# Pooled attention values accumulated onto the local ones in PSUM, for the jobs of the first batch half

## The chip, the cores and the metric

The kernel runs on one core of a Trainium2 chip. The metric is device time in microseconds for one execution, median of several runs. TensorE is called PE here, VectorE DVE, ScalarE ACT, GpSimd POOL; SP is the engine that issues the DMAs, from one queue that it works off in order. PE, DVE, ACT and POOL also run their own instructions in order.

## What is computed

Two attentions are added, and the sum goes through two feed-forward blocks. The attentions, from the reference (B = 2, H = 8, S = 576, D = 64, factor 4):

```python
q_d = q.reshape(B, H, Sd, factor, D).mean(axis=3)
...
out_d = sm_attn(q_d, k_d, v_d)
out_up = np.repeat(out_d, factor, axis=2)
...
out_local = np.matmul(attn, v)
return (out_up + out_local).astype(np.float32)
```

The pooled attention has 144 queries and keys, and each of its output rows is repeated for four neighbouring queries. The local attention sees keys less than four positions away. The sum, 1152 tokens of 512 channels, goes through `g = h * sigmoid(h); g @ w_out` (2048 hidden channels) and then through four experts of 1024 hidden channels, weighted by normalised `domain_probs`.

## The kernel before, in words

**Jobs.** Attention is cut into 16 jobs: two batches `b`, two chunks `c` of the sequence (256 and 320 queries, 4 and 5 blocks of 64), four pairs of heads `hp`. Jobs 0 to 7 are b = 0 (jobs 0 to 3 have 256 queries, jobs 4 to 7 have 320), jobs 8 to 15 are b = 1. After the fourth job of each batch a small tail job takes the last 16 pooled queries of all eight heads. A job goes through `local_scores`, `local_max`, `local_exp`, `down_scores`, `norm`, `trans`, `values` and `split_x`, one step a tick, three ticks a job.

**values and split_x.** `values` writes one PSUM tile `o`, of which there is one (`o_p`, bufs=1). Its columns 320 and up take the pooled result of 64 or 80 columns (line 408: four fp32 matmuls, two heads by two halves of the keys), its first 256 or 320 columns the local result (line 412: one fp32 matmul for each block and head). ACT copies the pooled part to SBUF with the factor 0.25 (`od`, line 415), DVE adds it onto the local part, each column for four queries (line 417). `split_x` then writes the sum in two parts for the feed-forward products, `xh` on ACT (line 424) and the rest `xl` on DVE (line 425), after which `o` is free for the next job.

**Weights.** The weights of the first feed-forward block come as 32 pieces of 512 KB through three staging buffers (`stg`, line 156). Two ACT instructions (lines 181 and 182) and two of DVE (183 and 187) decode a piece; DVE's line 187 is the last reader of its staging buffer. ACT then writes the upper part into `wbuf` (line 189), POOL the lower part (line 190). Twelve hidden-product tiles of a chunk need the first eight pieces; the second product of that chunk (`g2_step`) takes one more piece for each of its eight hidden blocks. These eight pieces are called f0 to f7 below; in the names of the order before they are stg64_546, 555, 564, 661, 670, 733, 753 and 789, in that of the order after stg64_537, 546, 555, 649, 658, 718, 738 and 774.

**Who sets the order.** The code gives each instruction a priority, and a scheduler of the framework sets the order of every engine's queue from the priorities and its own estimate of times. One instruction that changes its length or goes away can thus move others, on all queues, DMA issues among them.

**Products.** All products of the feed-forward blocks go through line 487 (first block, and the first product of the experts) and line 693. In the trace an fp32 matmul of the attention shows as two records, so four matmuls of line 408 are "x8" and eight of line 412 are "x16".

Of the kernel before, what the change touches and what calls it, by code (L numbers as in the profile page):

```python
# [15 lines left out]
ACTF = mybir.ActivationFunctionType  # L16
# [10 lines left out]
WIN = BQ + 6  # L27
# [32 lines left out]
def attention_moe_kernel(ctx, tc, kqa, kqb, qtl, va, vb, w64, w1d, w2d, dpr, out):  # L60
    nc = tc.nc
    PE, ACT, DVE, POOL, SP = nc.tensor, nc.scalar, nc.vector, nc.gpsimd, nc.sync
# [246 lines left out]
    def after(i, earlier):  # L309
        follow(i, earlier, "PSUM bank")  # L310
# [52 lines left out]
    def norm(j):  # L363
# [5 lines left out]
            DVE.tensor_tensor(out=j.sm, in0=j.lo, in1=j.st[:, 13:13 + nb].unsqueeze(2).to_broadcast([128, nb, WIN]), op=ALU.mult)  # L369
        ACT.activation(out=j.ed, in_=j.ed, func=ACTF.Copy, scale=j.st[:, 13 + nb:14 + nb])  # L370

    def trans(j):
        nb = j.nb
        if j.c == 1 and j.hp == 0:
            atd[j.b] = ac.tile([72, 2, NH, 80], F32, tag="atd1", name="atd1")
        t1 = t_p.tile([128, 4, 128], F32, tag="t1", name="t1")
        t2 = t_p.tile([128, 4, 128], F32, tag="t2", name="t2")
        j.at = ac.tile([WIN, 5, 128], F32, tag="at", name="at")
        for m in range(nb):
            PE.transpose(t1[0:WIN, m] if m < 4 else t2[0:WIN, 0], j.sm[:, m, :], ident)  # L380
        for kh in range(2):
            PE.transpose(t2[0:72, 1 + kh], j.ed[:, 72 * kh:72 * kh + 72], ident)
        ACT.activation(out=j.at[:, 0:4], in_=t1[0:WIN], func=ACTF.Copy)
        if nb == 5:
            ACT.activation(out=j.at[:, 4], in_=t2[0:WIN, 0], func=ACTF.Copy)
            dst = atd[j.b][:, :, 2 * j.hp:2 * j.hp + 2, 0:64]
        else:
            j.atd = ac.tile([72, 2, 2, 64], F32, tag="atd0", name="atd0")
            dst = j.atd
        ACT.activation(out=dst, in_=t2[0:72, 1:3].rearrange("p a (h q) -> p a h q", h=2), func=ACTF.Copy)  # L390

    def tail_trans(l):
        t2 = t_p.tile([128, 4, 128], F32, tag="t2", name="t2")
        for kh in range(2):
            PE.transpose(t2[0:72, 1 + kh], l.ed[:, 72 * kh:72 * kh + 72], ident)
        ACT.activation(out=atd[l.b][:, :, :, 64:80], in_=t2[0:72, 1:3].rearrange("p a (h q) -> p a h q", q=16),
                       func=ACTF.Copy)

    def values(j):
        b, hp, n, nb = j.b, j.hp, j.n, j.nb  # L400
        nd = n // 4
        o = o_p.tile([128, 512], F32, tag="o", name="o")
        v = vd[b, hp]
        for h in range(2):
            p = slice(64 * h, 64 * h + 64)
            for kh in range(2):
# [542 lines left out]
```

## Time and profile before

| | |
|---|---|
| median of 3 runs | 689.73 us (688.86 to 691.73) |
| profiled execution | 695.09 us, of which its span 693.1 us |
| PE busy | 658.0 us, 95% of the span |
| DVE busy | 441.9 us, 64% |
| ACT busy | 333.0 us, 48% |
| POOL busy | 247.2 us, 36% |
| mean granted PE clock | 0.974 of full |

The profile's page gives each engine's busy time; a view by stretches gives the same for parts of the span; the chain of waits follows the work that ended last back to the start; the view in order of time lists an engine's instructions, with the idle time before each and what ended it in brackets. A busy PE is not a PE at its peak: matmuls overlap, so the time that a run of them takes is read from the chain, where each piece lasts until the next one starts.

### The profile page before, as it was taken

Reading aid. Unit: us, or ns where it says so; the run is one execution under the profiler, and the core shown is the slowest. Engines: PE = TensorE matmul, PEld = TensorE weight load, DVE = VectorE, ACT = ScalarE, POOL = GpSimd, SP = SyncE. Lnnn points to the kernel's source line nnn. Section 1 sums busy time; section 2 is a strip of 40 time slices with the busy share of each in tenths; the row PEclk is TensorE's granted clock in tenths of the full one; section 3 lists DMA queues with packets and bytes.
Section 4 is the critical chain, followed back from the end, with each engine's and each line's share of the span. In section 5 each row is a group of like instructions: output and inputs, shape, how many; then the busy total and the mean of one; then the engine's idle time right before and its main releaser. Section 6 shows DMA issues by size and latency. Waiting matters only on the chain.

```text
span 693.1 us, 13803 instructions
## 1 busy us (share of the span) xinstructions
PE 658.0 (95%) x5516; PEld 641.0 (92%) x5516; DVE 441.9 (64%) x882; ACT 333.0 (48%) x753; POOL 247.2 (36%) x346
## 2 busy tenths in 40 slices
PE   5878779999999999999999999999999999999996
PEld 3758669998999999999999999999999999999996
DVE  5578967638564644585665985548855669756444
ACT  4659666647664533444335643345533356433321
POOL 5344762114240000154265432456232654322210
PEclk9597989999999999999999999999999999999999
DMA  9655553105250210022001410004310020000001
GB/s 288 203 160 173 168 178 99 27 7 152 93 183 1 61 62 2 1 100 115 1 2 53 130 61 1 1 2 122 92 31 1 1 61 1 1 32 17 16 31 45
DMA packets 16927, 48.16 MB, mean 69 GB/s; under 512 B 2976, under 2 KB 4256, under 8 KB 16864
## 3 DMA queue, kind: packets, MB, share of 16 engines
q1 hardware_dynamic: 16864, 47.29, 22.0%
q8 instruction: 43, 0.70, 0.4%
q14 instruction: 20, 0.16, 0.1%
HBM read 44.93 MB, written 2.36 MB: 68 GB/s over the span
## 4 chain that ended last, share of the span: by engine, by line
PE 83%; DMA 7%; DVE 6%; ACT 1%; POOL 1%; issue 1%; SPq 0%; ACTq 0%; POOLq 0%; DVEq 0%
PE mm L487 53%; PE p L693 26%; DMA stg<-in_w_dram 4%; DMA vg<-in_va_dram 2%; DVE dec L187 1%; DVE gl L513 1%; DVE dec L183 1%; PE s L320 1%; PE o L412 1%; PE t L380 1%; PE o L408 1%; DVE acc L721 1%; POOL vg L257 0%; PE s L344 0%; ACT stg L182 0%
## 5 line engine op out<-in xcount | busy, mean ns | idle before, releaser
L487 PE MATMUL mm<-xh,wbuf 128*128 128x256 f32 (+2 forms) x1280 | 268.9, 297 | 3.3 <-ACT xh L424 2.4
L487 PEld LDWEIGHTS mm<-xh,wbuf 128*128 128x128 f32 x1280 | 211.5, 190 | 4.1 <-ACT xh L424 3.0
L487 PE MATMUL mm<-xl,wbuf 128*128 128x256 f32 (+2 forms) x640 | 190.0, 297 | 0.0
L675 POOL TENSOR_TENSOR r<-r 128x128 f32<-128x128 f32 x160 | 93.4, 596 | 182.9 <-ACT r L669 143.3
L678 DVE TENSOR_TENSOR h<-r,h 128x384 fp32r<-128x384 f32 (+1 forms) x128 | 91.8, 719 | 64.0 <-ACT h L677 63.7
L487 PEld LDWEIGHTS mm<-xl,wbuf 128*128 128x128 f32 x640 | 121.7, 190 | 0.1
L677 ACT ACTIVATE h<-r 128x384 fp32r<-128x384 f32 (+1 forms) x128 | 73.3, 577 | 84.4 <-POOL r L675 54.3
L487 PE MATMUL mm<-gh,wbuf 128*128 128x256 f32 (+1 forms) x512 | 105.7, 298 | 6.2 <-ACT wbuf L189 3.3
L693 PE MATMUL p<-wext,h 128*128 128x256 f32 x672 | 91.5, 279 | 0.0
L487 PEld LDWEIGHTS mm<-gh,wbuf 128*128 128x128 f32 x512 | 83.1, 190 | 8.1 <-ACT wbuf L189 3.5
L693 PE MATMUL p<-wbuf,h 128*128 128x256 f32 x672 | 84.5, 278 | 0.0
L693 PEld LDWEIGHTS p<-wext,h 128*128 128x128 f32 x672 | 84.4, 188 | 0.0
L693 PEld LDWEIGHTS p<-wbuf,h 128*128 128x128 f32 x672 | 81.2, 188 | 0.0
L487 PE MATMUL mm<-gl,wbuf 128*128 128x256 f32 (+1 forms) x256 | 74.9, 297 | 1.2 <-DVE gl L513 1.2
L669 ACT ACTIVATE r<-mm 128x512 f32<-128x512 f32 x48 | 28.5, 597 | 76.0 <-PE mm L487 75.6
L675 DVE TENSOR_TENSOR r<-r 128x128 f32<-128x128 f32 x96 | 33.5, 350 | 37.7 <-ACT r L669 33.1
L487 PEld LDWEIGHTS mm<-gl,wbuf 128*128 128x128 f32 x256 | 48.6, 190 | 1.7 <-DVE gl L513 1.6
L513 DVE TENSOR_TENSOR gl<-gf,gh 128x256 fp32r<-128x256 f32 (+1 forms) x64 | 36.8, 580 | 17.2 <-ACT gh L512 16.0
L190 POOL TENSOR_TENSOR wbuf<-dec,wbuf 128x512 fp32r<-128x512 f32 x24 | 32.1, 1344 | 32.9 <-ACT wbuf L189 21.8
L721 DVE SCALAR_TENSOR_TENSOR acc<-p,pr,acc 128x256 f32<-128x256 f32 (+1 forms) x63 | 36.1, 604 | 5.9 <-PE p L693 5.9
L620 POOL TENSOR_TENSOR wext<-kst,wext 128x512 fp32r<-128x512 f32 x8 | 10.7, 1343 | 81.2 <-ACT wext L618 44.0
L507 DVE SCALAR_TENSOR_TENSOR gf<-th,mm 128x256 f32<-128x256 f32 (+1 forms) x64 | 28.3, 449 | 14.7 <-ACT th L506 13.7
(122 smaller groups left out, 978.2 us busy)
## 6 DMA issues: line engine op xcount, KB each, us to landing
stg<-in_w_dram SPq DMA_DIRECT2D x32, 512.0 KB, 4.3
kst<-in_w2d_dram SPq DMA_DIRECT2D x16, 512.0 KB, 3.8
kst<-in_w1d_dram SPq DMA_DIRECT2D x12, 512.0 KB, 3.7
kq<-in_kqa_dram SPq DMA_DIRECT2D x8, 419.0 KB, 3.6
kq<-in_kqb_dram SPq DMA_DIRECT2D x8, 323.0 KB, 9.5
vg<-in_va_dram SPq DMA_DIRECT2D x8, 288.0 KB
stg<-in_w1d_dram SPq DMA_DIRECT2D x4, 512.0 KB
vw<-in_vb_dram SPq DMA_DIRECT2D x8, 180.0 KB
```

The lines of the kernel that those rows point to most:

```text
L183: i = DVE.scalar_tensor_tensor(out=ai, in0=ai, scalar=3, in1=v[:, :, 0], op0=ALU.logical_shift_left, op1=ALU.bitwise_or)
L190: POOL.tensor_tensor(out=l[:, c], in0=a, in1=h[:, c].bitcast(F32), op=ALU.subtract)
L487: ins = [PE.matmul(out=ps, lhsT=l, rhs=r, start=(first and i == 0), stop=(last and i == n - 1)) for i, (l, r) in enumerate(pairs)]
L507: DVE.scalar_tensor_tensor(out=gf[:, 0:n], in0=th[:, 0:n], scalar=1.0, in1=ps[:, 0:n], op0=ALU.add, op1=ALU.mult)
L513: latest[DVE] = DVE.tensor_tensor(out=gl[ft][:, 0:n], in0=gf[:, 0:n], in1=gh[ft][:, 0:n].bitcast(F32), op=ALU.subtract)
L620: b = eng.tensor_tensor(out=l[:, r], in0=x, in1=h[:, r].bitcast(F32), op=ALU.subtract)
L669: ACT.activation(out=r[:, 0:4].rearrange("p s t -> p (s t)"), in_=ps[:, 0:512], func=ACTF.Relu)
L675: latest[eng] = eng.tensor_tensor(out=r[:, o], in0=r[:, a], in1=r[:, b], op=op)
L677: ACT.activation(out=h, in_=r[:, part], func=ACTF.Copy)
L678: latest[DVE] = DVE.tensor_tensor(out=l, in0=r[:, part], in1=h.bitcast(F32), op=ALU.subtract)
L693: ins = [PE.matmul(out=ps, lhsT=x, rhs=y, start=(opens and k == 0 and i == 0), stop=(k == 3 and i == n - 1), skip_group_check=True) for i, ...
L721: DVE.scalar_tensor_tensor(out=o, in0=ps, scalar=p, in1=o, op0=ALU.mult, op1=ALU.add)
```

## The change

For b = 0 the local products come first and open the sums in `o`, one start flag for each head. The pooled products then add onto the same columns: each pooled probability column is read four times by a broadcast access, so that the moving operand has 256 or 320 columns in place of 64 or 80. The factor 0.25 moves into the copy of the transposed probabilities (`pooled_scale`). The copy `od` and the DVE addition are left out, and `split_x` reads `o` as PE wrote it. For b = 1 the code is as before.

```diff
--- before.py
+++ after.py
@@ -368,6 +368,10 @@
             j.sm = a2.tile([128, nb, WIN], F32, tag="sm", name="sm")
             DVE.tensor_tensor(out=j.sm, in0=j.lo, in1=j.st[:, 13:13 + nb].unsqueeze(2).to_broadcast([128, nb, WIN]), op=ALU.mult)
         ACT.activation(out=j.ed, in_=j.ed, func=ACTF.Copy, scale=j.st[:, 13 + nb:14 + nb])
+
+
+    def pooled_scale(j):
+        return 0.25 if j.b == 0 else 1.0
 
     def trans(j):
         nb = j.nb
@@ -387,20 +391,41 @@
         else:
             j.atd = ac.tile([72, 2, 2, 64], F32, tag="atd0", name="atd0")
             dst = j.atd
-        ACT.activation(out=dst, in_=t2[0:72, 1:3].rearrange("p a (h q) -> p a h q", h=2), func=ACTF.Copy)
+        ACT.activation(out=dst, in_=t2[0:72, 1:3].rearrange("p a (h q) -> p a h q", h=2), func=ACTF.Copy,
+                       scale=pooled_scale(j))
 
     def tail_trans(l):
         t2 = t_p.tile([128, 4, 128], F32, tag="t2", name="t2")
         for kh in range(2):
             PE.transpose(t2[0:72, 1 + kh], l.ed[:, 72 * kh:72 * kh + 72], ident)
         ACT.activation(out=atd[l.b][:, :, :, 64:80], in_=t2[0:72, 1:3].rearrange("p a (h q) -> p a h q", q=16),
-                       func=ACTF.Copy)
+                       func=ACTF.Copy, scale=pooled_scale(l))
 
     def values(j):
         b, hp, n, nb = j.b, j.hp, j.n, j.nb
         nd = n // 4
         o = o_p.tile([128, 512], F32, tag="o", name="o")
         v = vd[b, hp]
+        if b == 0:
+            first = [None, None]
+            for m in range(nb):
+                for h in range(2):
+                    p = slice(64 * h, 64 * h + 64)
+                    i = PE.matmul(out=o[p, 64 * m:64 * m + 64], lhsT=j.vw[0:WIN, 128 * m + 64 * h:128 * m + 64 * h + 64],
+                                  rhs=j.at[:, m, p], start=(m == 0), stop=False, skip_group_check=True)
+                    if m == 0:
+                        first[h] = i
+                    else:
+                        after(i, first[h])
+            for kh in range(2):
+                for h in range(2):
+                    p = slice(64 * h, 64 * h + 64)
+                    r = j.atd[:, kh, h, :] if j.c == 0 else atd[b][:, kh, 2 * hp + h, :]
+                    PE.matmul(out=o[p, 0:n].rearrange("p (n r) -> p n r", r=4), lhsT=v[:, kh, p],
+                              rhs=r.unsqueeze(2).to_broadcast([72, nd, 4]), start=False, stop=(kh == 1),
+                              skip_group_check=True)
+            j.xf = o[:, 0:320]
+            return
         for h in range(2):
             p = slice(64 * h, 64 * h + 64)
             for kh in range(2):
```

The scheduler gives another order in all queues. Three places are shown: the load of f3, the end of the last pieces f6 and f7 (on SP and on ACT), and PE's queue behind f7. In the names, `mm` are the product tiles of line 487 (line 512 in the new file), `o` the tile of `values`, `kq`, `vw` and `vg` the loads of a job's keys and queries, windowed values and grouped values.

SP's queue, before, where job 13's keys (kq_1478) are loaded; stg64_661 is f3:

```order
L156 DMA stg64_555<-in_w64_dram 128x512
L156 DMA stg64_564<-in_w64_dram 128x512
L236 DMA kq_1351<-in_kqb_dram 128x646
L156 DMA stg64_661<-in_w64_dram 128x512
L236 DMA kq_1478<-in_kqb_dram 128x646
L156 DMA stg64_670<-in_w64_dram 128x512
```

The same place now; f3 is stg64_649:

```order
L156 DMA stg64_546<-in_w64_dram 128x512
L156 DMA stg64_555<-in_w64_dram 128x512
L244 DMA vw_729<-in_vb_dram 72x640
L236 DMA kq_1327<-in_kqb_dram 128x646
L236 DMA kq_1454<-in_kqb_dram 128x646
L156 DMA stg64_649<-in_w64_dram 128x512
L156 DMA stg64_658<-in_w64_dram 128x512
```

The load of f3 stood ahead of job 13's keys and now stands behind them, and behind job 6's windowed values (vw_729).

SP's queue, before, around the load of the first piece after f7 (stg64_858), which only the second half of the hidden channels needs:

```order
L244 DMA vw_882<-in_vb_dram 72x640
L156 DMA stg64_789<-in_w64_dram 128x512
L236 DMA kq_1076<-in_kqa_dram 128x838
L249 DMA vg_1288<-in_va_dram 72x1024
L156 DMA stg64_858<-in_w64_dram 128x512
L242 DMA vw_1027<-in_va_dram 72x512
L156 DMA stg64_891<-in_w64_dram 128x512
```

The same place now; that piece is stg64_840, and the next one stg64_873:

```order
L249 DMA vg_1264<-in_va_dram 72x1024
L156 DMA stg64_738<-in_w64_dram 128x512
L156 DMA stg64_774<-in_w64_dram 128x512
L242 DMA vw_1006<-in_va_dram 72x512
L156 DMA stg64_840<-in_w64_dram 128x512
L236 DMA kq_1055<-in_kqa_dram 128x838
L242 DMA vw_1156<-in_va_dram 72x512
L236 DMA kq_1202<-in_kqa_dram 128x838
L156 DMA stg64_873<-in_w64_dram 128x512
```

Between f7 and that piece stood a load of keys and one of grouped values; one load of windowed values stands there now. ACT's queue at the upper parts of f6 (dec_884) and f7 (dec_933), before:

```order
L181 ACTIVATE dec_933<-stg64_789 128x512
L182 ACTIVATE stg64_858<-stg64_858 128x512
L424 ACTIVATE xh_77<-o_961 128x320
L189 ACTIVATE wbuf_81<-dec_884 128x512
L390 ACTIVATE atd0_1218<-t2_1209 72x256
L189 ACTIVATE wbuf_81<-dec_933 128x512
```

And now, f6 as dec_866 and f7 as dec_915:

```order
L182 ACTIVATE stg64_840<-stg64_840 128x512
L189 ACTIVATE wbuf_81<-dec_866 128x512
L360 ACTIVATE ed_1050,st_973<-s_963,st_973 128x144
L449 ACTIVATE xh_77<-o_1083 128x320
L181 ACTIVATE dec_915<-stg64_774 128x512
L360 ACTIVATE ed_1197,st_1113<-s_1103,st_1113 128x144
L370 ACTIVATE ed_1050<-ed_1050,st_973 128x144
L181 ACTIVATE dec_2134<-stg64_840 128x512
L182 ACTIVATE stg64_873<-stg64_873 128x512
L394 ACTIVATE atd0_1194<-t2_1185 72x256
L387 ACTIVATE at_1186<-t1_1184 70x512
L189 ACTIVATE wbuf_81<-dec_915 128x512
```

f6 stands behind the decode of one piece past f7 as before; f7, which stood ahead of the decode of a second such piece, now stands behind it (stg64_873).

PE's queue, before, from the last products of f6 and f7 to the first product of the next block (mm_1182):

```order
L487 MATMUL mm_1151<-gl7_97,wbuf_81 128x256
L380 MATMUL t1_1333<-ident_118,sm_1263 70x128 x4
L320 MATMUL s_1393<-kq_1226 64x70 x8
L326 LDWEIGHTS ident16_119
L326 MATMUL s_1393<-mask_120,ident16_119 128x280
L382 MATMUL t2_1334<-ident_118,ed_1221 72x128 x2
L487 MATMUL mm_1031<-gh7_89,wbuf_81 128x256
L487 MATMUL mm_1078<-gh7_89,wbuf_81 128x256
L487 MATMUL mm_1151<-gh7_89,wbuf_81 128x256
L408 MATMUL o_1245<-atd0_1218,vd_1146 64x64 x4
L412 MATMUL o_1245<-at_1210,vw_1027 64x64 x8
L487 MATMUL mm_1182<-gh0_82,wbuf_81 128x256
```

And now, to mm_1158:

```order
L512 MATMUL mm_1127<-gl7_97,wbuf_81 128x256
L386 MATMUL t2_1310<-ident_118,ed_1197 72x128 x2
L384 MATMUL t1_1309<-ident_118,sm_1239 70x128 x4
L320 MATMUL s_1369<-kq_1202 64x70 x8
L326 LDWEIGHTS ident16_119
L326 MATMUL s_1369<-mask_120,ident16_119 128x280
L512 MATMUL mm_1010<-gh7_89,wbuf_81 128x256
L512 MATMUL mm_1057<-gh7_89,wbuf_81 128x256
L512 MATMUL mm_1127<-gh7_89,wbuf_81 128x256
L433 MATMUL o_1348<-atd0_1319,vd_1261 64x64 x4
L437 MATMUL o_1348<-at_1311,vw_1156 64x64 x8
L512 MATMUL mm_1158<-gh0_82,wbuf_81 128x256
```

Job 9's values (o_1348) now stand ahead of the next block, where job 8's (o_1245) stood; job 8's stand ahead of the products of f7.

## Rows read from the trace of the kernel before

**Rows 1.** Stretches: length, PE, PEld, DVE, ACT, POOL busy (instructions), PE clock, DMA share, GB/s.

```profile
34.60:52.00 17.40, 13.05 (x150) 10.27 (x148) 12.84 (x33) 9.01 (x24) 8.38 (x14) 0.93 0.52 160
52.00:69.00 17.00, 15.21 (x150) 14.32 (x149) 14.54 (x31) 15.39 (x43) 8.46 (x11) 0.77 0.57 170
69.00:86.00 17.00, 11.76 (x151) 10.26 (x151) 15.45 (x33) 11.20 (x29) 11.86 (x14) 1.00 0.56 170
86.00:104.00 18.00, 13.67 (x140) 11.55 (x139) 11.94 (x27) 11.11 (x30) 11.38 (x16) 0.81 0.60 180
104.00:121.00 17.00, 17.00 (x210) 15.58 (x208) 12.14 (x36) 10.86 (x32) 4.52 (x13) 1.00 0.34 100
```

**Rows 2.** Chain of waits, 82 to 105 us: start us, us, what.

```profile
82.99 8.81 DMA stg<-in_w_dram
...
91.82 0.65 ACT stg L182
...
92.80 0.53 ACT wbuf L189
...
93.37 1.31 PE mm L487 x6
...
102.34 2.27 PE mm L487 x18
```

**Rows 3.** Waits of PE, first 110 us: total us, times, longest.

```profile
PE mm L487 <- ACT wbuf L189: 3.3, 1, 3.3
```

**Rows 4.** DVE in order of time: start us, us, instruction, shapes.

```profile
69.56 0.49 DVE L417 TENSOR_TENSOR o<-o,od 128x320 f32<-128x320 f32 x1
69.96 0.16 DVE L365 TENSOR_SCALAR st<-st 128x6 f32<-128x6 f32 x1
...
71.85 3.32 DVE L187 SCALAR_TENSOR_TENSOR dec<-stg,dec 128x512 int32<-128x512 int32 x1
...
87.52 0.68 DVE L187 SCALAR_TENSOR_TENSOR dec<-stg,dec 128x512 int32<-128x512 int32 x1
...
93.24 0.68 DVE L187 SCALAR_TENSOR_TENSOR dec<-stg,dec 128x512 int32<-128x512 int32 x1
```

**Rows 5.** SP in order of time: start us, us, issue.

```profile
59.18 0.33 SPq L156 DMA_DIRECT2D stg<-in_w_dram  x1
63.25 0.33 SPq L236 DMA_DIRECT2D kq<-in_kqb_dram  x1
...
81.78 0.34 SPq L249 DMA_DIRECT2D vg<-in_va_dram  x1
...
88.26 0.33 SPq L156 DMA_DIRECT2D stg<-in_w_dram  x1
```

**Rows 6.** Chain of waits: values of a job, one fp32 matmul (L344).

```profile
94.68 0.74 PE o L408 x8
95.42 1.07 PE o L412 x20
...
104.61 0.24 PE s L344 x2
...
107.90 0.39 PE o L408 x8
108.29 0.47 PE o L412 x16
```

**Rows 7.** The copy and the addition, all 16 jobs: ns min/median/max.

```profile
L415 ACT ACTIVATE od<-o x16: 207/224/238, 29.2 to 150.3; 128x64 f32<-128x64 f32 x8, 128x80 f32<-128x80 f32 x8
L417 DVE TENSOR_TENSOR o<-o,od x16: 419/453/500, 29.5 to 150.5; 128x256 f32<-128x256 f32 x8, 128x320 f32<-128x320 f32 x8
```

**Rows 8.** Time from issue to landing of the weight pieces, first 175 us.

```profile
DMA to landing us min/median/max: 3.6/4.9/6.0
```

**Rows 9.** ACT in order of time: two copies of transposed probabilities.

```profile
86.41 0.58 ACT L383 ACTIVATE at<-t 70x512 f32<-70x512 f32 x1
...
87.04 0.38 ACT L390 ACTIVATE atd<-t 72x256 f32<-72x256 f32 x1
```

## The prediction, made before the changed kernel was run

> **What bounds the kernel now.** I read the view by stretches first [rows 1]. From 104 us PE is busy all the time (17.00 of 17 us), and so it is in nearly all that follows, since its 658.0 us fill 95% of the span. Before 104 us it is not: 13.05 of 17.4, 15.21 of 17, 11.76 of 17, 13.67 of 18 us, and the share counts matmuls at half clock (0.77, 0.81) as busy. So the kernel has an early part that waits for the weight pieces, and a long one that PE bounds. What the change is worth is how much earlier PE reaches the first product of the next block, from which on it never waits long.
>
> The chain of waits shows what sets that time [rows 2]. A piece that only the second half needs is issued at 82.99 and lands 8.81 us later. ACT decodes it (L182, 0.65), only then writes f6's upper part (L189, 0.53), and PE starts at 93.37. This was PE's one wait on L189 in 110 us, of 3.3 us [rows 3]. The wait is false: DVE had finished f6 by 88.20 (87.52 + 0.68) [rows 4], but ACT works in order and stood at a decode whose data had not come. Those had not come because SP had a load of keys and one of grouped values (81.78) just ahead [rows 5]. From 93.37 to the next block at 102.34 PE has 8.97 us of work: six products (1.31), then job 7's values, 0.74 + 1.07 at half clock [rows 6], then 5.85 us of products and of jobs 8 to 10.
>
> **PE's added work.** The pooled part had four matmuls of 64 or 80 columns; it now has four of 256 or 320. What a broadcast operand costs no row shows, so I bound it. Lower end: the local matmuls, whose two heads alternate as those of the new loop do, take 0.47 us for 8 of 64 columns, 0.92 ns a column [rows 6]; then 4 x 256 cost 0.94 us and 4 x 320 cost 1.18. Upper end: one fp32 matmul alone takes 0.24 us for 144 columns, 1.67 ns a column, hence 1.71 and 2.14 us. Less what they cost now (0.39 for 64 columns [rows 6], taken as 0.4 for 80), the eight jobs add 4 x 0.55 + 4 x 0.78 = 5.3 us by the lower end and 4 x 1.32 + 4 x 1.74 = 12.2 by the upper. I take the lower: the same shapes of output, 64 partitions by turns, stand in that row, and L408, which goes head by head, is the slow one there (0.39 for 256 columns). All eight jobs lie ahead of the next block. PE idles 18.3 us in the four stretches up to 104 us [rows 1], so this is costed at nothing. Without that cover it would be 5.3. Only the last two jobs may stand in the way: serial matmuls would cost 2 x (2.14 - 1.18) = 1.9 us there.
>
> The Trainium skill ("TensorE: Matmul & The Clock Gate", Part 3, What overlaps and what doesn't) says that a weight load overlaps with running matmuls only where the row groups differ. The two heads share their rows here, so that rule would put the new loop at the serial end. The row on the alternating matmuls, 0.92 against 1.67 ns a column, speaks against it.
>
> **What goes.** Eight additions on DVE and eight copies on ACT [rows 7]. From its start to the next instruction's an addition takes 0.40 us (69.56 to 69.96) [rows 4]. Two more stand at 81.37 and 87.14, so three lie where DVE is nearly full (15.45 of 17 us from 69 to 86 [rows 1]): 1.2 us of DVE's queue ahead of f6 and f7. The copies are 224 ns each, with ACT busy for 11.20 of 17 us there; nothing is counted for them. `o` comes free some 0.7 us earlier a job (0.22 + 0.45), which matters only where PE waits for it, and no wait of that kind stands in the chain.
>
> **What moves.** (a) *f3's load.* It stood at 59.18 and now stands behind job 13's keys, issued at 63.25 [rows 5]: up to 4.07 us later. ACT's queue stops at its landing, and exponentials of the attention stand behind that decode. Cover: PE idles again by 5.24 us from 69 to 86, DVE is 1.2 us shorter, and f4 and f5 wait for a staging buffer rather than for SP. I take it as made up by f6: net 0, bounds -1.2 (DVE's share alone) and +4.07.
>
> (b) *f6.* The piece past f7 is now issued behind one load of windowed values, at about 82.6. It lands the median 4.9 us later [rows 8] (3.6 to 6.0 for those that the view matched; the 8.81 of the chain lies outside), 87.5. With L182 and L189 f6 is out by 88.7, while DVE is ready at 88.20. So f6's six products and job 7's values, 1.31 + 1.81 = 3.12 us, go ahead of f7, into time in which PE waited.
>
> (c) *f7.* It was written right behind f6. Now ACT decodes a second piece past f7 first, and two attention copies stand between. That piece needs the staging buffer that f6's L187 frees at 88.20; before, its load was issued at 88.26 [rows 5]. It lands at 88.26 + 4.9 = 93.16. Then L182 0.65, two copies 0.58 + 0.38 [rows 9], L189 0.53: f7 is out at 95.3. DVE's side of f7 ended at 93.92 in the run before only because the queue ahead of it waited for ACT [rows 4]; it is no limit now. A load of keys stands just ahead of the piece, as one did ahead of the 8.81 us, so the bounds of the landing are 3.6 and 8.81: f7 out between 94.0 and 99.2.
>
> (d) *Behind f7* PE has the same work as in the 5.85 us, with job 9's values in place of job 8's. Job 9's (0.39 + 0.47 = 0.86 us [rows 6]) came behind the next block's first product before. So the time before to compare with is 102.34 + 0.86 = 103.20. At the same clock the new time is 95.3 + 5.85 = 101.15.
>
> **Sum.** 103.20 - 101.15 = 2.05 us earlier. The bounds of (c) alone give 3.35 earlier to 1.86 later. The profiled execution took 695.09 us (span 693.1 and 2.0 around it), 5.4 above the median of the runs; it would take 693.0. I put the same difference on the median: 689.73 - 2.05 = **687.7 us**. Not in it: the last job of b = 1 now ends 24 products later, 24 x 2.27/18 = 3.0 us of PE's work [rows 2]. No row shows a wait at that end; half of it, 1.5, goes to either side of the range.
>
> **The rivals.** *Full clock, early pieces: 684.4 to 685.6.* Before, the granted clock was 0.81 from 86 to 104 us [rows 1], and the pieces of the chain show half clock in the 4.2 us from 96.48 to 100.7: a full clock there saves 2.1. For it: PE has work longer, with the wider matmuls and job 8's values in time where it stood idle. Against it: it still waits for f7. With the sum 689.73 - 4.15 = 685.6, and with DVE's 1.2 as well 684.4. The Trainium skill (same page, Part 1) says that the throttled clock is the default and activity releases it; the extra columns would be a help by that rule, and the rows before 52 us, 0.93 at 13.05 of 17.4 us, do not exclude it.
>
> *f3 comes late and stays late: 691.8 to 695.7, slower.* Each piece holds a buffer, so a late f3 can push f4 to f7. Price: the 4.07 of the issue, and if the load lands behind the keys as slowly as the one of 8.81 did, 3.91 more: 687.7 + 4.07 = 691.8 up to 687.7 + 7.98 = 695.7. It is slower than before from 2.05 us that are not made up. For it: DVE has 1.55 us free in 69 to 86, so it cannot catch up much. Against: PE's idle time there, and the buffers.
>
> *The landing for f7 is the slow one: 691.6.* 8.81 in place of 4.9, thus 99.2 + 5.85 = 105.06 against 103.20. For it: the load of keys just ahead. Against: before, two big loads stood there, now one.
>
> *Unpaired matmuls: 689.6.* The broadcast read or the shared rows give 1.67 ns a column; 1.9 of the 2.05 are lost.
>
> *A collision: 690.3.* One L187 took 3.32 us where the others take 0.68 [rows 4]; POOL was working on a piece at the same time. If a moved order makes one more, on f6 or f7, 2.64 go. The Trainium skill ("SBUF — State Buffer", Who interferes with whom) gives a shared port: a DVE instruction with two inputs from SBUF contends with POOL's reads. L187 is one; the addition that goes reads PSUM, so its removal frees no port by that rule.
>
> That the change does not do what it says can be left out: the new queues hold the wide matmuls and no `od`.
>
> **How the numbers follow.** Chances: forecast 0.38, full clock 0.25, f3 0.14, slow landing 0.10, unpaired 0.08, collision 0.05. A measurement tells about 0.5%, 3.45 us. Faster by more (below 686.3): most of the full clock, 0.21, the better third of the forecast, 0.14, and 0.01 of the rest, 0.36. Slower by more (above 693.2): 0.09 of f3, 0.03 of the slow landing, 0.04 of the others' spread, 0.16. Between: 0.48. The range goes from the full clock less 1.9 of spread, 682.5, to the middle of f3's case, 693.5, and leaves out about 0.07 below and 0.13 above.
>
> **What would show it.** In the new profile: wide pooled matmuls at 0.94 and 1.18 us a job (serial: 1.71 and 2.14); f6's L189 near 88.7 and f7's near 95; PE's wait before the first product of f7, not of f6; the next block's first product near 101. A wait on f3's piece around 67 us that PE still feels behind 86 us would prove (a) wrong; a next block at 105 would prove (c) wrong; a gain or loss that arises behind 104 us would prove wrong that only the early part counts.

## The result, and the profile after

The changed kernel is slower: 699.01 us median (696.62 to 701.36) against 690.13 us (688.86 to 691.73; six executions of each, where the 689.73 above is the median of three), a ratio of 1.0122, interval 1.0092 to 1.0153. The forecast was 687.7 us with a range up to 693.5; time and direction were both missed.

Fifteen runs followed. One of them (e11) is the kernel before once more, profiled in an execution of 690.51 us. Its trace stands for the typical execution below, since the first one, at 695.09 us, turned out to be late in the very stretch on which the forecast rested. The profile of the changed kernel, in turn, is of the slowest of its six executions, 701.36 us, 2.4 above its median.

The view by stretches of the changed kernel (columns as in [rows 1]):

```profile
34.60:52.00 17.40, 17.16 (x162) 12.94 (x158) 9.17 (x25) 6.92 (x20) 7.34 (x13) 1.00 0.42 126
69.00:86.00 17.00, 14.07 (x125) 10.92 (x122) 16.39 (x31) 10.90 (x30) 10.47 (x11) 0.82 0.50 155
86.00:104.00 18.00, 16.89 (x179) 12.04 (x178) 13.11 (x30) 13.59 (x33) 12.05 (x18) 0.98 0.72 234
104.00:121.00 17.00, 17.00 (x178) 15.82 (x179) 10.60 (x29) 9.82 (x29) 6.17 (x15) 1.00 0.23 71
121.00:160.00 39.00, 39.00 (x422) 36.52 (x420) 20.41 (x59) 20.87 (x64) 5.62 (x11) 1.00 0.10 29
160.00:200.00 40.00, 35.88 (x270) 34.73 (x269) 28.77 (x47) 28.22 (x61) 13.59 (x11) 1.00 0.41 131
```

And of e11, the kernel before in a typical execution:

```profile
34.60:52.00 17.40, 13.52 (x173) 10.64 (x170) 13.53 (x35) 8.64 (x25) 8.27 (x14) 0.97 0.61 183
69.00:86.00 17.00, 11.73 (x145) 10.15 (x145) 16.68 (x34) 11.20 (x29) 10.44 (x13) 1.00 0.55 177
86.00:104.00 18.00, 15.90 (x189) 13.94 (x185) 13.43 (x32) 13.98 (x39) 15.15 (x20) 1.00 0.75 228
160.00:200.00 40.00, 39.64 (x288) 38.54 (x288) 28.39 (x45) 28.36 (x60) 15.67 (x12) 1.00 0.47 145
```

Two things stand out. In the three stretches shown up to 104 us PE is busier than in e11, as the wide products want, and it is no earlier for it (from 52 to 69 us it is busy for 14.42 us, e11's for 15.33). And from 160 to 200 us, a stretch of which the prediction made no term, PE is idle for 4.1 us of 40 where the typical execution before is idle for 0.4.

The chain of waits of the changed kernel before the next block (start us, us, what), which answers to [rows 2]:

```profile
94.69 5.07 DMA vg<-in_va_dram
...
99.90 1.27 POOL vg L257
101.17 1.01 POOL kq L257 x2
102.17 1.24 POOL wbuf L190
...
103.46 0.62 PE mm L512 x3
...
104.93 3.02 PE mm L512 x24
```

And of e11 at the same place:

```profile
84.36 6.48 DMA stg<-in_w_dram
...
90.86 0.68 ACT stg L182
...
98.61 2.39 PE mm L487 x18
```

The next block starts at 98.61 in the typical execution, at 102.34 in the first one [rows 2], and at 104.93 in the changed kernel. Of the load that took 8.81 us there, 6.48 are left in e11, and PE's wait on L189, 3.3 us [rows 3], is 1.0.

The end of the attention in ACT's view in order of time, e11 first, then the changed kernel:

```profile
147.46 0.44 ACT L424 ACTIVATE xh<-o 128x320 fp32r<-128x320 f32 x1 [0.56 <-DVE o L417]
147.83 1.15 ACT L189 ACTIVATE wext<-dec 128x512 fp32r<-128x512 f32 x2
```

```profile
156.42 0.44 ACT L449 ACTIVATE xh<-o 128x320 fp32r<-128x320 f32 x1
156.75 1.14 ACT L189 ACTIVATE wext<-dec 128x512 fp32r<-128x512 f32 x2
```

`xh` is the last job's sum; `wext` takes the first weights of the second half of the hidden channels. In the code both are tied together: `wext` lies in the memory that the attention leaves.

```python
actx.close()
late = ctx.enter_context(tc.tile_pool(name="late", bufs=1))
wext.append(late.tile([128, 4 * KF], F32R, name="wext"))
```

So the second half's weights start 8.92 us later (156.75 against 147.83), and the span is 10.8 us longer (699.3 against 688.5). The rows do not tell a wait for that memory from the place in ACT's queue, where `wext` stands right behind `xh`.

### The profile page after: what moved, and what is told of

The parts are those of the page before. It is cut to its first block, busy times and chain, and to the rows that moved or that the text cites. A ratio compares the mean times of both kernels' runs of the same rounds, so it can differ in the third digit from the quotient of the medians.

```text
span 699.3 us, 13782 instructions
## 1 busy us (share of the span) xinstructions
PE 669.8 (96%) x5516; PEld 644.1 (92%) x5516; DVE 438.4 (63%) x874; ACT 329.9 (47%) x745; POOL 246.6 (35%) x346
## 4 chain that ended last, share of the span: by engine, by line
PE 82%; DMA 6%; DVE 5%; issue 2%; ACT 2%; POOL 2%; SPq 0%; POOLq 0%; ACTq 0%; DVEq 0%
PE mm L512 51%; PE p L718 25%; DMA stg<-in_w_dram 5%; DVE dec L187 1%; DMA vg<-in_va_dram 1%; DVE dec L183 1%; PE s L320 1%; POOL wbuf L190 1%; PE o L424 1%; PE t L384 1%; PE s L284 1%; PE s L344 1%; PE o L437 1%; DVE acc L746 1%; ACT stg L182 0%
## 5 line engine op out<-in xcount | busy, mean ns | idle before, releaser
L538 DVE TENSOR_TENSOR gl<-gf,gh 128x256 fp32r<-128x256 f32 (+1 forms) x64 | 32.7, 516 | 17.5 <-ACT gh L537 14.7
L645 POOL TENSOR_TENSOR wext<-kst,wext 128x512 fp32r<-128x512 f32 x8 | 10.8, 1345 | 81.6 <-ACT wext L643 43.2
```

Of the source, the lines that this page charges most:

```text
L538: latest[DVE] = DVE.tensor_tensor(out=gl[ft][:, 0:n], in0=gf[:, 0:n], in1=gh[ft][:, 0:n].bitcast(F32), op=ALU.subtract)
L645: b = eng.tensor_tensor(out=l[:, r], in0=x, in1=h[:, r].bitcast(F32), op=ALU.subtract)
```

## The experiments

The order of all five queues can be held: a table in the kernel names the order, and each instruction is tied to the one ahead of it on its engine, without a wait (`ORDER` is the table, packed). "Old order" and "new order" are those of the kernel before and of the changed one.

### Order or work: e1 and e2

```diff
+    for n, keys in json.loads(zlib.decompress(base64.b85decode(ORDER))).items():
+        seq = [by[n, k] for k in keys if (n, k) in by]
+        for x, y in zip(seq, seq[1:]):
+            follow(y, x, "given order")
```

**e1.** 

> The changed kernel's work (local products first, wide pooled products added in PSUM, no copy od, no addition) with every engine's queue, SP's included, held to the order of the kernel before; in a job's place for its values the local products stand ahead of the pooled ones. Theory A (the loss comes from the order that the scheduler gave, not from the work): no slower than the kernel before, 688 to 691 us, perhaps 1 us faster for the eight additions. Theory B (the wide products, at half clock in the first jobs and in the chain of the attention, cost the time): 694 to 699 us.

**e2.** 

> The kernel before's work (narrow pooled products, copy od, addition on DVE) in the order of the changed kernel on every engine; local products ahead of the pooled ones for b = 0, od right behind them on ACT, the addition one to four instructions ahead of xl on DVE. Theory A (order): 697 to 701 us, as slow as the changed kernel. Theory B (work): 689 to 692 us.

e1 took 695.63 us, ratio 1.0055 (1.0024 to 1.0086); e2 698.46 us, 1.0135 (1.0070 to 1.0200). The old work in the new order is as slow as the changed kernel (1.0122); the new work in the old order loses less than half of that. Theory A holds for the larger part: the order, not the work. e1's 0.55% is more than A allowed, and its 695.63 us lies in the range of B; it is e2 that speaks against B, which gave it 689 to 692.

### Which half of the order: e3 and e4

Both kernels differ from e1 in their table alone, which changes over at the next block's first product. In e3's trace the values of jobs 10 to 15 stand behind 248 to 393 products, as in the changed kernel, in e4's behind 229 to 369, as in the kernel before.

**e3.** 

> The changed kernel's work; up to the first product of the next block (near 103 us) in the order of the kernel before, behind it in the order of the changed kernel. Theory A1 (the order behind 104 us: the last attention jobs of b = 1 stand 24 products later, and the weights of the second half wait for the memory that they leave): 694 to 699 us. Theory A2 (the order ahead of the next block: weight pieces behind loads of keys): 688 to 691 us. Theory B (work): 694 to 699 us.

**e4.** 

> The changed kernel's work; up to the first product of the next block in the order of the changed kernel, behind it in that of the kernel before. Theory A1 (order behind 104 us): 688 to 692 us. Theory A2 (order ahead of the next block): 695 to 699 us. Theory B (work): 694 to 699 us.

e3: 699.16 us, 1.0120 (1.0068 to 1.0171). e4: 697.85 us, 1.0113 (1.0063 to 1.0163). Both are nearly as slow as the changed kernel, so A1 and A2 each hold in part. Both carry the new work too, which alone cost 0.55% in e1: beyond that the late half costs 0.65 points and the early half 0.58. With e1's 0.55 that makes 1.8 where the changed kernel has 1.22; with intervals of 0.3 to 0.5 points on each, whether they add up is open. ACT of e3, in order of time, shows the late half:

```profile
157.62 0.44 ACT L277 ACTIVATE xh<-o 128x320 fp32r<-128x320 f32 x1
157.96 1.14 ACT L277 ACTIVATE wext<-dec 128x512 fp32r<-128x512 f32 x2
```

(In kernels with a held order all instructions carry the line of the helper that records them; the tile's names tell them apart.) In e4 the last xh comes at 155.80, for the other reason: PE's 175th product starts at 108.31 there, against 99.42 in e11, and the old order behind it makes little up.

### The end of the attention alone: e5, e6, e7

```diff
-            prio(tick[0] - (0 if f in main_parts else LEAD_ATTN))
+            prio(tick[0] - (0 if f in main_parts else 9 if args and getattr(args[0], "b", 0) else LEAD_ATTN))
```

**e5.** 

> The kernel before with one number changed: the lead that the priorities give the attention jobs of b = 1 is 9 in place of 11. The first fifteen jobs keep their places; the last job's values stand behind 390 products in place of 369 (the changed kernel: 393). Theory A1 (the weights of the second half go into the memory that the attention leaves, so the last job's end sets when their decoding starts, and PE then waits for them): the last xh about 3 us later than 151.07, PE level up to 170 us and 3 to 5 us late at 200 us, the time 693 to 696 us, 2 to 5 us above the kernel before. Rival (the end of the attention is covered; the loss came from the order of the decoding itself or from the wide products): within 1 us of the kernel before.

e5: 694.67 us, 1.0070 (1.0051 to 1.0088). The end of the attention on ACT, in order of time:

```profile
151.16 0.44 ACT L424 ACTIVATE xh<-o 128x320 fp32r<-128x320 f32 x1 [0.19 <-DVE o L417]
151.54 1.15 ACT L189 ACTIVATE wext<-dec 128x512 fp32r<-128x512 f32 x2
```

PE was ahead of e11 by 3.9 us at the 375th product (143.39 against 147.32) and behind it by 5.1 at the 575th (177.01 against 171.90). Fifteen jobs stand where they stood before; the last one ends 3.7 us later than in e11, and the span is 4.3 us longer (692.8). The expected cost of 2 to 5 us is met; that the last xh would be late against the first profile's 151.07 was not, because that number was itself late.

The run does not show that the cost is a wait for the second half's weights. Two other things came with the new place of the last job. PE's queue takes its local products by turns with six products of line 487, from 146.16 to 150.26 us, where its local products take 0.60 us in one piece in e11. And the granted clock was half, 0.50, from 149.2 to 155.9 us and from 173.1 to 176.4, where e11 has 1.00. What each is worth is open; no run separates them.

**e6.** 

> The changed kernel with the lead of the attention jobs of b = 1 at 13 in place of 11: the last job's values stand behind 356 products in place of 393. Theory A1: the last xh at 150 to 152 us in place of 156.42, the loss of 5 us between 170 and 200 us goes, and the time is 690 to 694 us. Rival (wide products, or the order ahead of the next block): 696 to 699 us, as the changed kernel.

**e7.** 

> The kernel before with the lead of the attention jobs of b = 1 at 13: the last job's values stand behind 346 products in place of 369. Theory A1: if the end of the attention still bounds the start of the second half's weights, 2 to 3 us faster than before, 687 to 689 us; if PE no longer waits there, within 1 us. Rival (the end of the attention does not matter): within 1 us as well, so this run only counts if it gains.

e6: 706.24 us, 1.0239 (1.0206 to 1.0273). e7: 696.19 us, 1.0094 (1.0069 to 1.0119). Both missed. Fewer products ahead of the last job did not bring its end forward: the last xh came at 162.26 in e6 and at 151.09 in e7. In e6 12.2 us pass between the 175th and the 200th product (110.41 to 122.65; 3.4 us in e11): PE waits for job steps there, and the view by stretches gives a granted clock of 0.80 from 104 to 124 us. These are waits of PE in e6, 86 to 130 us (engine and line, waited for: us in total, times, longest):

```profile
PE t L384 <- DVE sm L369: 2.4, 1, 2.4
...
PE o L433 <- DVE xl L450: 1.0, 1, 1.0
```

Neither run speaks for or against A1, since the thing that was to come earlier came later; they show that the lead is no knob for it.

### The wide products: e8

```diff
-                    PE.matmul(out=o[p, 0:n].rearrange("p (n r) -> p n r", r=4), lhsT=v[:, kh, p],
-                              rhs=r.unsqueeze(2).to_broadcast([72, nd, 4]), start=False, stop=(kh == 1),
+                    PE.matmul(out=o[p, 0:nd], lhsT=v[:, kh, p], rhs=r, start=False, stop=(kh == 1),
```

**e8.** 

> As e1 (the changed kernel's work in the order of the kernel before) with the pooled products narrow: 64 or 80 columns, added onto the first columns of the sums. Three quarters of the pooled additions are left out. The difference to e1 is the price of the wide products in that order. Theory B2 (the wide products cost what e1 lost, 3.8 us): 690 to 692 us, at most as slow as the kernel before. Rival (what e1 lost comes from the locals standing ahead of the pooled products, or from the spread of the runs): 694 to 697 us, as e1.

e8: 694.09 us, 1.0040 (1.0010 to 1.0071), against e1's 1.0055. The difference is 0.15%, 1 us, and within both intervals. From the two intervals its own is about 3 us to either side (estimate), so the wide columns, 5.3 us of PE's work by the prediction, may have cost nothing or all of what e1 lost. Theory B2's 690 to 692 us missed and the rival's 694 to 697 holds, by a little; the run leans against the columns and does not settle it.

### Moving the end of the attention forward by hand: e9, e10, e12; and e11

Again the table alone holds another order. In the traces of e9 and e12 the values of jobs 9 to 15 stand behind 204, 223, 241, 267, 292, 317 and 346 products (208 to 369 in the kernel before), in e10's behind 240, 264, 290, 315, 341 and 370 for jobs 10 to 15 (248 to 393 in the changed kernel).

**e9.** 

> The kernel before's work in its own order, but from product 174 on every instruction of the attention of b = 1 and of the first two weight units of the second half (loads, ACT, DVE, POOL, PE) is moved ahead of the products, by a share that grows to 24 products at the last job: its values stand behind 346 products in place of 369. Theory A1 (the end of the attention frees the memory for the second half's weights, and sets when they can be decoded): the last xh about 3 us earlier in relation to the products, the time 2 to 4 us below the kernel before, 686 to 688 us. Rival (the end of the attention is covered): within 1 us of the kernel before.

**e10.** 

> The changed kernel in its own order, with the same shift from product 174 on: the last job's values stand behind 370 products in place of 393, where the kernel before has them; nothing ahead of the next block is changed. Theory A1: 2 to 4 us faster than the changed kernel, 695 to 697 us. Rival A2 (the loss arises ahead of the next block): 698 to 700 us, as the changed kernel.

**e11.** 

> The kernel before once more, for its profile. The first profile was of an execution 5.4 us above the median. If that excess lay ahead of the next block (a long landing of 8.81 us and a wait of 3.3 us that this execution had and others have not), the first product of the next block comes 4 to 7 us earlier, at 96 to 99 us, as in e5, whose order is the same up to there. If those rows are of every execution, it comes at 102 to 104 us again.

**e12.** 

> As e1 (the changed kernel's work in the order of the kernel before) with the shift of e9. Theory A1: 2 to 4 us faster than e1 was, 690 to 693 us. Rival (the end of the attention is covered): as e1, 694 to 697 us.

e9: 697.83 us, 1.0110 (1.0072 to 1.0149). e10: 699.10 us, 1.0133 (1.0097 to 1.0169). e12: 698.37 us, 1.0147 (1.0089 to 1.0206). All three missed what Theory A1 gave them; e10 lies in its rival's 698 to 700. In e9 PE began to wait for the attention's own chain; from 100 to 152 us it is busy for 47.51 of 52 us, against 52.00 in e11, and these are PE's waits there (engine and line, waited for: us in total, times, longest):

```profile
PE o L278 <- DVE xl L278: 1.9, 2, 1.1
PE s L278 <- ACT od L278: 1.2, 1, 1.2
PE s L278 <- ACT s L278: 0.8, 1, 0.8
```

The last xh came at 150.08, later than in e11. The old order has no slack of 24 products there: by these waits, the jobs of b = 1 already follow each other about as closely as `o`, `s` and the softmax allow. In e10 the last xh came 1.3 us earlier (155.13) and the profiled span was 3.0 shorter (696.3), but the median did not fall. The late loss did go there: from the 500th to the 675th product PE took 23.7 us, as in e11 (23.6), where the changed kernel took 28.2. But PE reached the 500th 3.6 us later than the changed kernel (171.67 against 168.06), so the loss moved ahead of it.

e11 started the next block's first product at 98.61, within the 96 to 99 us of the first forecast, though 3.7 us earlier and not 4 to 7: most of the excess of the first profile lay there. Its PE is 3.7 us ahead of the first profile at the 175th product and 4.6 at the 1200th.

### One part of the change alone: e13 and e14; the order within a job: e15

```diff
-        if b == 0:
+        if b == 0 and j.c == 1:       # e13: jobs 4 to 7; e14: j.c == 0, jobs 0 to 3; pooled_scale likewise
```

**e13.** 

> The change for jobs 4 to 7 only, with the scheduler's own order; the last job's values stand behind 345 products. Theory C (the loss ahead of the next block comes from the values of jobs 0 to 2, since the decoding of the first weights is tied to the end of job 2): the two pieces that wait for job 2 are written near 47 us as before, the next block starts at 97 to 104 us, and the time is 688 to 693 us. Rival (any change of these jobs brings an order that is slow): 695 to 699 us.

**e14.** 

> The change for jobs 0 to 3 only, with the scheduler's own order; the last job's values stand behind 353 products. Theory C: the two pieces that wait for job 2 are written at 50 us or later, the next block starts at 104 to 108 us, and the time is 694 to 699 us. Rival (the loss comes from jobs 4 to 7): 688 to 693 us.

**e15.** 

> The kernel before's work in its own order on every engine, except that in jobs 0 to 7 the local products stand ahead of the pooled ones in the places of a job's values on PE. Theory D (the local products wait longer, for the windowed probabilities, than the pooled ones do, and that costs e1 and e8 their 3 to 4 us): 692 to 695 us. Rival (no price for that order; e1 and e8 are slow for another reason): within 1.5 us of the kernel before.

e13: 697.26 us, 1.0128 (1.0072 to 1.0184). e14: 697.43 us, 1.0108 (1.0055 to 1.0162). e15, which swaps two loops of `values` under the old order: 692.66 us, 1.0021 (0.9994 to 1.0047). That lies at the low end of Theory D and 1.7 us above the kernel before in the same session, so it decides nothing on D; it does bound what the holding of an order costs by itself.

e14's time went as Theory C says; its two pieces were written at 48.82 and 49.91, a little before the 50 us of the forecast, and its next block started at 108.17, a little behind 104 to 108. The code ties the first decoding of the second weight unit to the last vector instruction of job 2:

```python
if u in behind_job:
    follow(i, behind_job[u], "first weights")
```

These are DVE's xl of job 2 and the decoding behind it, and ACT's write of the two pieces, in the views of both engines in order of time (start us, length us, what it waited for in brackets). In e11:

```profile
43.77 0.41 DVE L425 TENSOR_TENSOR xl<-o,xh 128x256 fp32r<-128x256 f32 x1
44.11 0.68 DVE L183 SCALAR_TENSOR_TENSOR dec<-dec,stg 128x512 int32<-128x512 int32 x1
```

```profile
47.30 1.23 ACT L189 ACTIVATE wbuf<-dec 128x512 fp32r<-128x512 f32 x2 [1.40 <-DVE dec L187]
```

In the changed kernel:

```profile
47.63 0.42 DVE L450 TENSOR_TENSOR xl<-o,xh 128x256 fp32r<-128x256 f32 x1
48.03 1.28 DVE L183 SCALAR_TENSOR_TENSOR dec<-dec,stg 128x512 int32<-128x512 int32 x2
```

```profile
50.38 0.63 ACT L189 ACTIVATE wbuf<-dec 128x512 fp32r<-128x512 f32 x1 [0.91 <-DVE dec L187]
51.46 0.63 ACT L189 ACTIVATE wbuf<-dec 128x512 fp32r<-128x512 f32 x1 [0.45 <-DVE dec L187]
```

Job 2 ends 3.9 us later in the changed kernel than in e11, and the weight pieces behind it stay late: f0 is written at 67.45 in place of 62.10, f7 at 99.80 in place of 93.00.

The rows also show a reason for job 2's delay: PE's clock. Two products one behind the other, in PE's view in order of time, in e11 and then in the changed kernel:

```profile
35.62 0.28 PE L487 MATMUL mm<-xh,wbuf 128*128 128x256 f32 x1
35.74 0.28 PE L487 MATMUL mm<-xl,wbuf 128*128 128x256 f32 x1
```

```profile
40.34 0.42 PE L512 MATMUL mm<-xh,wbuf 128*128 128x256 f32 x1
40.56 0.42 PE L512 MATMUL mm<-xl,wbuf 128*128 128x256 f32 x1
```

The second starts 0.12 us after the first in e11, at full clock (2.4 GHz), and 0.22 us after it in the changed kernel, at half (1.2 GHz). The clock records of these two traces begin with the rise to full, at 33.76 us in e11 and at 42.21 in the changed kernel; the view by stretches counts the time ahead of the first record as full, hence the 1.00 of its row from 34.6 us. From 25 us to the rise PE had no gap of over 0.3 us in either. Half of the 8.45 us between the two rises, 4.2 us of PE's work (estimate), covers the 3.9. And this belongs to the order: from 34.5 to 41.3 us products follow each other mostly at 0.21 us in all six runs whose early order is new (the changed kernel, e2, e4, e6, e10, e14), at 0.12 in the eleven others. Why PE gets its full clock later in that order no run shows. Nor is job 2 all of it: in e2 it ends at 45.32, 1.6 us behind e11's, and f0 is 4.5 us late (66.63), since 21.3 us pass between the two, 18.3 in e11.

e13 leaves these rows alone (xl at 43.55, the pieces at 47.08) and yet has the time of the others; its forecast of 688 to 693 us missed. It is 0.6 us behind e11 at the 150th product (88.57 against 87.98) and 5.7 at the 200th (108.53 against 102.80): around there PE waits for a job's step and for a weight piece (waits of PE, 86 to 130 us):

```profile
PE t L386 <- ACT ed L370: 2.3, 1, 2.3
PE mm L512 <- ACT wbuf L189: 1.8, 1, 1.8
```

Another piece of the order went wrong there, at the next block. So Theory C fits the early loss of the changed kernel and e14, with the clock as the likely reason for job 2's delay, and not every slow order.

### All profiled executions side by side

| run | ratio | last xh, us | span, us | difference |
|---|---|---|---|---|
| e11, kernel before again | 1 | 147.46 | 688.5 | 541.0 |
| kernel before, first profile | 1 | 151.07 | 693.1 | 542.0 |
| changed kernel | 1.0122 | 156.42 | 699.3 | 542.9 |
| e1 new work, old order | 1.0055 | 151.99 | 695.5 | 543.5 |
| e2 old work, new order | 1.0135 | 158.39 | 697.9 | 539.5 |
| e3 old early, new late | 1.0120 | 157.62 | 697.7 | 540.1 |
| e4 new early, old late | 1.0113 | 155.80 | 698.7 | 542.9 |
| e5 last job later | 1.0070 | 151.16 | 692.8 | 541.6 |
| e6 new, lead 13 | 1.0239 | 162.26 | 706.6 | 544.3 |
| e7 old, lead 13 | 1.0094 | 151.09 | 694.7 | 543.6 |
| e8 narrow | 1.0040 | 148.59 | 692.4 | 543.8 |
| e9 old, shift | 1.0110 | 150.08 | 696.6 | 546.5 |
| e10 new, shift | 1.0133 | 155.13 | 696.3 | 541.2 |
| e12 new work, old order, shift | 1.0147 | 150.29 | 695.2 | 544.9 |
| e13 jobs 4 to 7 | 1.0128 | 149.57 | 693.2 | 543.6 |
| e14 jobs 0 to 3 | 1.0108 | 154.58 | 700.2 | 545.6 |
| e15 locals first | 1.0021 | 149.97 | 691.4 | 541.4 |

Each row's span is of one execution, and those of one kernel differ by up to 9 us (e14: 693.44 to 702.09). The last xh moves over 14.8 us and the span over 18.1, while the difference stays within 539.5 to 546.5. That does not make the end of the attention the cause: the start of PE's 375th product does as well, with 540.4 to 545.0 us from there to the end of the span in 15 of the 17 runs. It fails in two whose last job comes late, the changed kernel (547.5) and e5 (549.4).

What tells a late last job apart is PE's time from its 500th to its 675th product: 26.6 to 28.2 us in the four runs whose last job's values stand behind 390 products or more (changed kernel, e2, e3, e5), 23.1 to 25.1 in the 13 others. So an order with a late last job costs PE some 3 to 4 us behind the attention; by which link is taken up next.

## Why the prediction was wrong, point by point

**What bounds the kernel.** Half right. PE does bound the time from 104 us to the end of the attention (17.00 of 17 us up to 121 in both, 39.00 of 39 up to 160 in the changed kernel). The step that failed is "from which on it never waits long". In the changed kernel PE is level with the first profile at the 500th product (168.06 against 168.32) and 4.7 us late at the 675th (196.26 against 191.58). Its longest wait in that stretch, with ACT's rows ahead of it, both in order of time:

```profile
175.24 0.68 ACT L182 ACTIVATE stg<-stg 128x512 int32<-128x512 uint16 x1 [1.02 <-DMA stg<-in_w_dram]
175.81 0.64 ACT L564 ACTIVATE acc<-mm 128x256 f32<-128x256 f32 x2
176.23 0.38 PE L512 MATMUL mm<-gh,wbuf 128*128 128x256 f32 x1 [2.00 <-ACT acc L564]
```

PE waited 2.00 us until ACT had copied a finished product tile out (`acc`), and ACT stood at a decode of weights whose load had not landed. The same wait is 1.94 us in e5, 1.76 in e2 and 1.51 in e3, the other three with a late last job. In the 13 other traces PE has no wait for `acc` from 150 to 205 us.

How the last job's place leads to this wait is not shown in full. In the chain of waits of the kernel before, which the prediction did not follow that far, the end of the attention leads to the second half's weights:

```profile
151.07 0.02 ACT xh L424
...
151.45 0.64 ACT wext L189
```

In that of the changed kernel neither `xh` nor this first write of `wext` stands. It goes through the products behind the last job's values, on to ACT's next step of the feed-forward block, `th`, and the decode behind it:

```profile
155.52 3.30 PE mm L512 x27
...
158.90 0.39 ACT th L531
159.28 0.57 ACT dec L181
```

So the memory that the attention leaves is a link in one kernel's chain, as far as queue and memory can be told apart there, and in the other ACT's queue and PE's products are.

**The base of the sum.** The sum went against 102.34 us, where the 8.81 us landing and the 3.3 us wait stand [rows 2, 3]. The text noted that this execution was 5.4 us above the median and put "the same difference on the median", as if it were spread evenly. e11 shows 3.7 of it at the next block's start. A wait that was largely this execution's own was counted as something that the change removes. The cause named for it was misread as well: the load issued at 82.99 did not stand behind SP's two loads, the last of them issued at 81.78, but followed DVE's L187 (81.86 to 82.93 in the chain), which frees a staging buffer.

**PE's added work.** Right for a block at full clock that the order leaves whole. One of 1024 columns lasts from 45.87 to the next product at 46.83, 0.96 us (estimate 0.94), one of 1280 columns 1.23 us (estimate 1.18); the serial 1.71 and 2.14 did not occur. PE of the changed kernel in order of time (start us, length us), then two blocks of its chain of waits (start us, us):

```profile
45.87 1.04 PE L424 MATMUL o<-atd,vd 72*64 72x256 f32 x8
46.83 0.39 PE L344 MATMUL s<-kd,qbd 128*128 128x144 f32 x1
```

```profile
35.88 1.91 PE o L424 x8
...
68.73 1.23 PE o L424 x8
```

That the idle time hides it is not settled: e8 against e1 leaves 1 us of the 5.3, with about 3 to either side. The idle time of the four stretches adds up to 15.7 us by [rows 1], not to 18.3. Not foreseen was the half clock of the first jobs, 1.91 us for job 1's block, nor that the order would split a block: job 7's two parts take 0.63 and 1.22 us. The rival with unpaired matmuls falls; the Trainium skill's rule on weight loads ("TensorE: Matmul & The Clock Gate", Part 3, What overlaps and what doesn't) did not hold for the two heads here, by the 0.96 us.

**What goes.** Eight additions and copies went, as said (the third of the three additions counted, at 87.14, lies behind the stretch up to 86 us). No run shows a gain from it: with the old order (e1) the kernel is slower, not faster.

**(a) f3's load.** The delay came, but not by SP's queue: f0 is already 5.3 us late (67.45 against 62.10), behind job 2 and its half clock, and f3 4.5 (81.10 against 76.57). "Made up by f6" was wrong. The slower rival had the right sign (2.1 to 6.0 us slower, where 8.9 were measured), for another reason.

**(b) f6.** Wrong: 94.27 in place of 88.7, in ACT's view in order of time:

```profile
94.27 0.63 ACT L189 ACTIVATE wbuf<-dec 128x512 fp32r<-128x512 f32 x1 [0.16 <-DVE dec L187]
...
99.80 0.64 ACT L189 ACTIVATE wbuf<-dec 128x512 fp32r<-128x512 f32 x1
```

The false wait that the change was to remove went, but the piece was not there in time.

**(c) f7.** Predicted 95.3, measured 100.4 (99.80 + 0.64), and then not ACT but POOL came last: f7's lower part stood behind the folding of grouped values that landed at 99.76 (the chain above), and f7's products started right behind it, at 103.46. PE did work of the attention until 103.36, so it lost 0.1 us there in idle time; its one wait for POOL's weights up to 104 us, 1.8 us, ended at 79.18, before f6 and f7. The slow landing did not come: the load issued at 94.31 had landed by 98.48. The prediction named ACT's queue and SP's; POOL's, in which that load now holds up the weights, it left out. The prediction's own sign of a wrong (c), a next block at 105, came (104.93).

**(d) and the 24 products.** The sentence on b = 1 had the mechanism's first half, "the last job of b = 1 now ends 24 products later", and priced it at 1.5 us to either side because "no row shows a wait at that end". It is a term that was mis-sized: e3, which adds the new late order to e1, costs 4.5 us more than e1 (1.0120 less 1.0055, with intervals of 0.5 and 0.3 points), and e5, with 21 products, 4.8 us by its ratio, part of which may be its clock and its split block.

**The other rivals.** The full clock came, 0.98 from 86 to 104 us, but e11 has 1.00 there without the change, so it was no gain of it. The collision did too, and as before: one L187 of 3.27 us at 81.95 in the changed kernel, one of 3.35 in e11.

**Open.** The new work in the old order is slower by 0.55% (e1), with narrow products by 0.40% (e8), and the swapped loops alone by 0.21%, which is not clear of nothing (e15). Where the 2.8 to 3.8 us of e8 and e1 come from (0.40 and 0.55% of 690) is not settled. Nor is what made the scheduler choose the new order: no run changed its estimates alone. That `wext` waits for its memory, rather than for its place in ACT's queue, is read from the code and was not tried; nor was the clock of the first 42 us. No order of the new work was found that beats the kernel before, and none of the old work either.

## What to carry to other kernels

Where a scheduler sets the order, price an edit by the new order first: the same work in another order moved this kernel by 0.7 to 1.4%, more than the edit's own work did. Then follow the chain past the point where the busiest engine looks full: here the loss behind 104 us came back as one wait of 2.00 us for an engine that stood at a late load. And ask of every row that carries a sum whether it is the kernel's or that execution's: an execution above the median has its excess somewhere, and one more profile shows where.

## What the runs showed of the hardware that was not expected

A moving operand that reads each column four times by broadcast runs at the rate of a dense one: 0.94 ns a column for two heads by turns (0.96 us for 1024), as the local products' 0.92 [rows 6]. The order of the queues moved PE's rise to its full clock, from 33.76 us (e11) to 42.21 (changed kernel), with PE busy from 25 us on in both. The same program differs between executions by more than expected in its early part: with identical queues up to there, the 175th product started at 96.68 (e5), 99.42 (e11) and 103.07 us (first profile), with the load ahead of it landing in anything from 6.48 (e11) to 8.81 us.
